# Weight halves, two written-out groups and another order of attention work in a fused attention and two-stage feed-forward kernel

## The chip, the cores and the metric

The kernel runs on one core of one Trainium2 chip. The metric is device time in microseconds (us) of one execution, as the median of several. Engines: TensorE (PE, its weight loads are PEld), VectorE (DVE), ScalarE (ACT), GpSimd (POOL) and the queue engine SyncE (SP), which starts transfers.

## The reference

Three computations follow each other, all in 32-bit floats, with the second kind of weights given as 64-bit words that the kernel turns into floats itself.

```python
# attention: batch 2, 8 heads, 768 positions, head size 64
scores = q @ k.T / sqrt(64) - slope[head] * distance
scores = where(key < n_global or 0 <= query - key < n_local, scores, -1e9)
a = softmax(scores); x = a @ v              # x: 1536 tokens x 512
# first feed-forward: 512 -> 2048 -> 512
h = x @ w_in; g = where(h > 0, h, exp(min(h, 0)) - 1); x = g @ w_out
# second feed-forward: 512 -> 768 -> 512
out = max(x @ w1, x @ w2, x @ w3) @ w_out2
```

## The kernel before, in words

**Precision.** Each large matrix product is done as three products of rounded operands: high by high, high by low and low by high part. So every operand is split into a high part (a cast, on ScalarE) and a low part (a subtraction, mostly on VectorE).

**Attention steps.** The attention is cut into 48 steps (k = 0 to 47): two heads, 128 queries, a window of at most 232 keys. `Windowed` (L117) holds their pieces: `scores_pe` (L214, products on TensorE into banks S0 and S1), `scores_dve` (L239, bias and minimum on VectorE), `scores_act` (L268, exponentials and sums on ScalarE), `sums` (L234), `recip` and `norm` (L263, L280, VectorE), `turn_pe` (L290, four transposes on TensorE into a bank), `turn_act` (L307, copy of the transposes to SBUF), `values_pe` (L318, products with the values). The finished values leave the bank by `values_high` and `values_low` (steps 0 to 15), by `pair_pe` and `pair_out` (two steps at once), or by `due_pe` and `due_out` (the steps that `due` names; for an even k these are k-3 and k-2).

**Weights.** The hidden layer of 2048 is cut into 16 groups of 128 (fc). The 64-bit words of a group (its columns of w_in and its rows of w_out, 2 x 512 words per partition) are turned into floats by six instructions: `c_rebase` (ScalarE), `c_low` (VectorE), `c_word` twice (VectorE), then the high part by `c_high` (ScalarE) and the low part by `c_rest` (VectorE). Here they are called rebase, low, word, word, high and rest. Half 0 is the w_in part and feeds the first product, half 1 the w_out part and feeds the output products. The last two groups arrive as separate halves.

**First stage.** `windowed` (L1182) runs steps 0 to 15 in a loop (L1221), which makes the first block of 512 tokens. From step 8 on each step also advances `convert`, a hand-written list of weight instructions for groups 0 and 1. In the steps named in `FILL` (L43) TensorE does that many identity products (`fill`, L759) whose result nobody reads. Behind the loop an epilogue written out by hand finishes steps 14 and 15, starts steps 16 and 17, and does the first product of group 0 in pieces.

**Main loop.** `run` (L765) then goes over three blocks of 512 tokens and in each over the 16 groups. In group fc TensorE does the product into bank h (`product`, 12 matmuls), some attention work of step k, and the output products of the group before (`out_high` 8 matmuls, `out_low` 4 matmuls, into banks y0 to y3). ScalarE and VectorE make e from h (`elu_exp`, `elu_max`) and split it into gh and gl (`high`, `low`). There is one bank h in blocks 0 and 1: the next product may start only when `elu_max` has read the last one. Step k goes with group k - 18: steps 18 to 33 with block 0, 34 to 47 with block 1, and block 2 has none. In block 0 the weights of group fc + 1 and fc + 2 are unpacked between the other instructions.

**What sets the order.** Nothing reorders the work: each engine takes its instructions in the order in which the program calls the methods above (a manual schedule), and waits where a tile isn't ready or a buffer not yet free. The eight PSUM banks are single tiles under the names h, S0, S1, TX and y0 to y3; a new tile in a bank waits for the last reader of the one before. Two tiles gl and gh, one tile e. In `run`, `joint` (L787) decides which of two orders a group uses for the attention step: if not joint, transposes of step k-1 directly behind the product, and values as pairs; if joint, `due_pe` directly behind the product, and the transposes later.

Of the kernel before, what the change touches and what calls it, by code (L numbers as in the profile page):

```python
# [12 lines left out]
F32 = mybir.dt.float32  # L13
# [5 lines left out]
ALU = mybir.AluOpType  # L19
# [5 lines left out]
P = 128  # L25
NB = S // P
NCC = DM // P
NFC = FF // P
# [370 lines left out]
class Feed:  # L399
# [54 lines left out]
    def c_rebase(self, c):  # L454
        for r, _ in self.parts(c):
            a = r[..., 1].bitcast(F32)
            self.nc.scalar.activation(a, a, AF.Copy, scale=2.0 ** -112)

    def c_low(self, c):
        for r, _ in self.parts(c):  # L460
# [4 lines left out]
    def c_word(self, c, n):  # L465
        v, op = ((3, ALU.logical_shift_left), (0x80000000, ALU.bitwise_and))[n]
        for r, _ in self.parts(c):
# [4 lines left out]
    def c_high(self, c):  # L472
        for r, h in self.parts(c):
            if c not in self.w:
                self.w[c] = self.wt.tile([P, 2, 2, 512], F32R, tag="w", name="w")
            self.nc.scalar.copy(self.w[c][:, h, 0], r[..., 0].bitcast(F32))  # L476

    def c_rest(self, c):
        for r, h in self.parts(c):
            w = self.w[c]  # L480
            self.nc.vector.tensor_tensor(
                w[:, h, 1], r[..., 0].bitcast(F32), w[:, h, 0].bitcast(F32), op=ALU.subtract
            )
        for d, k in ((self.whole, c), (self.wraw, 2 * c), (self.wraw, 2 * c + 1)):
            if c < NFC:
                d.pop(k, None)
# [277 lines left out]

    def run(self, at, k, x=None, h0=None, aside=None):  # L765

        nc, ps = self.nc, self.ps
# [7 lines left out]
        for bi, n in enumerate(BLOCKS):  # L777
            prev = y = None
            for fc in range(NFC):
                tag = ("h", "S0")[fc % 2] if k >= len(at.steps) + 2 else "h"  # L780
                if h0 is None:
                    h = ps.tile([P, 512], F32, tag=tag, name="h")[:, 0:n]
                    self.product(h, self.w[fc][:, 0], x, n, order=BEHIND if bi == 0 else None)
                else:
                    h, h0 = h0[:, 0:n], None
# [10 lines left out]
                if bi == 0:  # L796
                    self.c_word(fc + 1, 1)
                if left:
                    self.out_low(*left)
                late = bi == 0 or fc > 0  # L800
                if not late:
                    at.turn_act(k - 1, nc.vector.tensor_copy)
                    if k % 2 == 0:
                        at.pair_pe(k - 2)
                    at.scores_dve(k)
                    e = self.elu_exp(h, n)
                    at.scores_act(k)
                    if k % 2 == 0:
                        at.pair_out(k - 2, nc.scalar.copy)
                else:  # L810
                    ahead = bi == 0 and fc == NFC - 1
                    behind = joint and due and (ahead or k == len(at.steps))
                    if ahead:
                        at.scores_dve(k)
                        at.scores_act(k)
                        at.sums(k)
                        at.recip(k)
                        at.norm(k)
                    e = self.elu_exp(h, n)
# [4 lines left out]
                    if bi == fc == 0:  # L824
                        at.turn_act(k - 2, nc.scalar.copy)
# [4 lines left out]
                sooner = bi == 0 and (fc == 0 or k % 2)  # L830
                if sooner:
# [30 lines left out]
                if bi == nblk - 1 and fc == 7:  # L862
                    next(sums, None)
                if due and not behind:
                    at.turn_act(k - 1, nc.scalar.copy)
                if late and bi:
# [3 lines left out]
                    at.norm(k)  # L870
                if k % 2 == 0 and bi == fc == 0:
                    at.pair_pe(k - 2)
                    at.pair_out(k - 2, nc.scalar.copy)
                left = None
# [10 lines left out]
                if k % 2 == 0 and not joint and bi + fc:  # L885
                    at.pair_pe(k - 2)
                    at.pair_out(k - 2, nc.scalar.copy)
# [12 lines left out]
                k += 1  # L900
                prev = gh, gl
            if bi + 1 < nblk:
                t = [t] + [at.take(g0 + i) for i in range(1, BLOCKS[bi + 1] // GRP)]
# [278 lines left out]
def windowed(tc, ctx, io, flag):  # L1182
# [5 lines left out]
    with tc.manual_schedule():  # L1188
# [12 lines left out]
        def convert():  # L1201
            f.c_rebase(0)
            f.c_low(0)
            yield
            f.c_word(0, 0)
            f.c_rebase(1)
            yield
            f.c_word(0, 1)
            yield
            f.c_high(0)  # L1210
            f.c_low(1)
            yield
            f.c_rest(0)
            yield
            f.c_word(1, 0)
            yield
# [171 lines left out]
```

## Time and profile before

| | |
|---|---|
| Runs | 542.35, 542.89 and 542.96 us; median 542.89 |
| The profiled execution's own time | 542.19 us |
| Its span, first to last instruction | 540.4 us |
| Busy: TensorE, weight loads, VectorE, ScalarE, GpSimd | 530.7, 426.8, 393.7, 288.0, 82.9 us |
| Granted TensorE clock, mean over the span | 0.998 |
| First stage (steps 0 to 15 and epilogue) | about 0 to 44 us |
| Block 0, block 1, block 2 of the main loop | about 44 to 152, to 262, to 348 us |
| Second feed-forward | to 535 us |

In the lists of the profile a row gives a start, a duration, engine, line of the kernel, operation, written and read tiles, shapes and a count; a bracket at its end is the time that the engine sat idle before and who released it. Times are us from the span's start. A row's duration contains the start and the end of its instruction and overlaps with the next row of the same engine by some 0.08 to 0.1 us, so what an instruction costs its queue is read from one start to the next. The ends of matmuls are modelled. A fp32 product counts as two records.

### The profile page before, as it was taken

The numbers are of one execution on the slowest core, as the hardware profiler recorded it, in microseconds if no ns is written. First come the engines' busy times: TensorE is split into PE (matmuls) and PEld (weight loads), VectorE is DVE, ScalarE is ACT, GpSimd is POOL, SyncE is SP. The second block draws the span as 40 slices with busy tenths as digits, with TensorE's granted clock in tenths as the row PEclk, the third lists the DMA queues.
The fourth block names the chain that finished last, engine by engine and source line by source line (L and its number), as shares of the span: only waits on it lengthen the run. The fifth ranks groups of instructions, "written<-read, shape, count | busy, mean of one in ns | idle before, by whom it ended". The sixth has DMA issues, their size and how long they took to land.

```text
span 540.4 us, 7751 instructions
## 1 busy us (share of the span) xinstructions
PE 530.7 (98%) x2746; PEld 426.8 (79%) x2746; DVE 393.7 (73%) x828; ACT 288.0 (53%) x649; POOL 82.9 (15%) x89
## 2 busy tenths in 40 slices
PE   8999999999999999999999999999999999999995
PEld 6667787777777888888888888888888888888884
DVE  6889999999854444443567656787886989779883
ACT  5979877888845555554545655552157321224020
POOL 4220000000000000000000044321034410335000
PEclk9999999999999999999999999999999999999999
DMA  8929055442310111000000031331029301876014
GB/s 284 397 95 409 21 196 196 156 161 83 101 46 24 45 44 44 21 19 1 0 2 0 1 117 40 116 115 42 1 71 308 146 1 40 270 293 234 1 73 168
DMA packets 23455, 59.21 MB, mean 110 GB/s; under 512 B 2416, under 2 KB 2416, under 8 KB 23408
## 3 DMA queue, kind: packets, MB, share of 16 engines
q1 hardware_dynamic: 18368, 49.46, 26.5%
q10 hardware_dynamic: 5040, 9.18, 4.5%
q8 instruction: 24, 0.39, 0.3%
q14 instruction: 23, 0.19, 0.1%
HBM read 49.19 MB, written 9.44 MB: 108 GB/s over the span
## 4 chain that ended last, share of the span: by engine, by line
PE 91%; DVE 5%; ACT 3%; issue 0%; POOL 0%; ACTq 0%; POOLq 0%
PE h L674 26%; PE y L705 16%; PE y L713 8%; PE y L975 8%; PE y L1069 5%; PE y L674 5%; PE S L975 4%; PE TX L327 3%; PE TX L304 3%; PE S L228 3%; PE S L1069 2%; PE TX L975 2%; PE S L674 2%; PE h L975 2%; PE TX L1069 2%; ACT p L275 1%
## 5 line engine op out<-in xcount | busy, mean ns | idle before, releaser
L674 PE MATMUL h<-xh,w 128*128 128x512 f32 (+1 forms) x432 | 122.2, 387 | 0.2 <-ACT w L476 0.2
L705 PE MATMUL y<-gh,w 128*128 128x512 f32 x384 | 98.7, 399 | 0.1
L510 POOL TENSOR_TENSOR w<-wr,w 128x512 fp32r<-128x512 f32 x42 | 62.9, 1507 | 231.8 <-ACT w L509 220.5
L674 PEld LDWEIGHTS h<-xh,w 128*128 128x128 f32 x432 | 80.2, 188 | 17.9 <-ACT w L476 0.8
L705 PEld LDWEIGHTS y<-gh,w 128*128 128x128 f32 x384 | 69.7, 188 | 14.3 <-issue 0.5
L674 PE MATMUL h<-xl,w 128*128 128x512 f32 (+1 forms) x216 | 71.0, 386 | 0.0
L699 DVE SCALAR_TENSOR_TENSOR e<-e,h 128x512 f32<-128x512 f32 x48 | 32.9, 685 | 49.5 <-ACT e L695 49.4
L509 ACT CAST w<-wr 128x512 fp32r<-128x512 f32 x42 | 27.6, 663 | 63.4 <-DVE wr L500 51.1
L694 ACT ACTIVATE e<-h 128x512 f32<-128x512 f32 x48 | 28.7, 599 | 55.3 <-PE h L674 51.2
L275 ACT ACTIVATE p<-p,m 128x232 f32<-128x232 f32 (+1 forms) x96 | 44.9, 471 | 17.1 <-DVE m L254 16.9
L713 PE MATMUL y<-gl,w 128*128 128x512 f32 x192 | 51.6, 390 | 0.0
L500 DVE SCALAR_TENSOR_TENSOR wr<-wr 128x512 uint32<-128x512 uint32 x48 | 44.2, 921 | 7.5 <-ACT wr L492 6.0
L686 DVE TENSOR_TENSOR gl<-e,gh 128x512 fp32r<-128x512 f32 x48 | 33.1, 689 | 19.9 <-ACT gh L681 19.9
L674 PEld LDWEIGHTS h<-xl,w 128*128 128x128 f32 x216 | 40.4, 188 | 8.1 <-issue 0.2
L198 POOL TENSOR_SCALAR raw<-raw,qsc 128x256 f32<-128x256 f32 x24 | 16.8, 699 | 193.4 <-DMA raw<-qk 193.4
L975 PE MATMUL y<-t,w 128*128 128x512 f32 x180 | 42.7, 389 | 0.0
L713 PEld LDWEIGHTS y<-gl,w 128*128 128x128 f32 x192 | 36.0, 188 | 8.0 <-issue 0.3
L681 ACT CAST gh<-e 128x512 fp32r<-128x512 f32 x48 | 29.6, 616 | 23.5 <-DVE e L699 23.3
L468 DVE SCALAR_TENSOR_TENSOR wr<-wr 128x1024 uint32<-128x1024 uint32 (+1 forms) x36 | 39.8, 1120 | 0.4
L975 PEld LDWEIGHTS y<-t,w 128*128 128x128 f32 x180 | 33.8, 188 | 7.0
L695 ACT ACTIVATE e<-e 128x512 f32<-128x512 f32 x48 | 30.3, 632 | 1.5
L985 ACT CAST g<-m 128x512 fp32r<-128x512 f32 x18 | 10.9, 621 | 35.2 <-DVE m L1004 27.0
(155 smaller groups left out, 837.5 us busy)
## 6 DMA issues: line engine op xcount, KB each, us to landing
wr<-wa SPq DMA_DIRECT2D x14, 1024.0 KB, 6.9
wr<-wb SPq DMA_DIRECT2D x24, 512.0 KB, 4.6
v<-v SPq DMA_DIRECT2D x24, 256.0 KB, 2.8
part<-row ACTq DMA_DIRECT2D x24, 256.0 KB, 4.6
raw<-qk SPq DMA_DIRECT2D x16, 312.0 KB, 4.6
row<-part SPq DMA_DIRECT2D x12, 256.0 KB, 3.1
out<-rows ACTq DMA_DIRECT2D x11, 256.0 KB, 2.3
raw<-qk SPq DMA_DIRECT2D x8, 260.0 KB, 4.7
```

The lines of the kernel that those rows point to most:

```text
L275: self.nc.scalar.activation(p[:, o], p[:, o], AF.Exp, bias=m[:, u:u + 1], scale=-1.0, accum_out=m[:, 2 + u:3 + u],)
L468: self.nc.vector.scalar_tensor_tensor(r[..., 0], r[..., 1], v, r[..., 0], op0=op, op1=ALU.bitwise_or)
L500: self.nc.vector.scalar_tensor_tensor(t, a, c, t, op0=op, op1=ALU.bitwise_or)
L510: nc.gpsimd.tensor_tensor(w[:, u, 1], v, w[:, u, 0].bitcast(F32), op=ALU.subtract)
L674: nc.tensor.matmul(out[:, o:n], w[:, part % 2, c * P:c * P + P], (xl if part == 2 else xh)[:, c, o:n], start=(c, part) == order[0], stop=( ...
L686: (engine or self.nc.vector).tensor_tensor(gl[:, 0:n], e[:, 0:n], gh[:, 0:n].bitcast(F32), op=ALU.subtract)
L695: self.nc.scalar.activation(e, e, AF.Exp, scale=-1.0)
L699: self.nc.vector.scalar_tensor_tensor(e, e, -1.0, h, op0=ALU.add, op1=ALU.max)
L705: self.nc.tensor.matmul(y[e][:, 0:n], w[:, a, e * P:e * P + P], g[0][:, 0:n], start=fc == 0 and a == 0, stop=False,)
L713: self.nc.tensor.matmul(y[e][:, 0:n], w[:, 0, e * P:e * P + P], g[1][:, 0:n], start=False, stop=fc == NFC - 1,)
L975: self.nc.tensor.matmul(out, w[:, u, i % 2, b + c * P:b + c * P + P], o[:, i // 2, c], start=c == i == 0, stop=c == 1 and i == 2,)
L1069: nc.tensor.matmul(o, t[:, a, r], w[:, u, b], start=u == k == 0, stop=u == 1 and k == 2,)
```

## The change

It has four parts.

1. `FILL`: one identity product in place of two in each of steps 8 to 13.
2. The methods `c_...` take a half h. `convert` now unpacks half 0 of groups 0 and 1 first and of half 1 of group 0 only the first instructions; it has eight pieces, one for each of steps 8 to 15. The other pieces of half 1 stand in the epilogue and in `begin`.
3. `begin` is new: groups 0 and 1 of the first block written out by hand in place of the first two turns of the loop in `run`. The product of group 1 goes to bank y3; its first four matmuls stand before the transposes of step 17, the other eight behind them. `run` begins at group 2 with step 20.
4. `joint` is now true for every group of blocks 0 and 1 (before: for groups 2 to 15 of each block). What changes by it are groups 0 and 1 of block 1: the values of step 32 alone directly behind the product, scores, and then the transposes of step 33.

```diff
-FILL = {1: 2, 2: 2, 8: 2, 9: 2, 10: 2, 11: 2, 12: 2, 13: 2}
+FILL = {1: 2, 2: 2, 8: 1, 9: 1, 10: 1, 11: 1, 12: 1, 13: 1}
...
-    def parts(self, c):
-
+    def parts(self, c, h=None):
+
+        hs = slice(0, 2) if h is None else slice(h, h + 1)
         if c in self.whole:
-            return [(self.whole[c], slice(0, 2))]
+            return [(self.whole[c][:, hs], hs)]
         return [(self.wraw[j], j % 2) for j in (2 * c, 2 * c + 1) if j in self.wraw and c < NFC]
...
-    def c_low(self, c):
-        for r, _ in self.parts(c):
+    def c_low(self, c, h=None):
+        for r, _ in self.parts(c, h):
             self.nc.vector.tensor_scalar(
...
+    def begin(self, at, k, x, h):
+
+
+        copy, n = self.nc.scalar.copy, BLOCKS[0]
+        w = self.w[1][:, 0]
+        at.load_values(k)
+        self.w_ahead(4)
+        at.scores_pe(k, m=2)
+        at.turn_pe(k - 2, "y2")
+        h1 = self.ps.tile([P, 512], F32, tag="y3", name="h1")
+        self.product(h1, w, x, n, 0, 0, 4, BEHIND)
+        at.recip(k - 1)
+        at.norm(k - 1)
+        self.c_low(1, 1)
+        at.turn_pe(k - 1)
+        self.product(h1, w, x, n, 0, 4, 8, BEHIND)
+        e = self.elu_exp(h, n)
+        at.turn_act(k - 2, copy)
+        at.turn_act(k - 1, copy)
+        self.elu_max(e, h)
+        at.scores_dve(k)
+        gh = self.high(e, n)
+        gl = self.low(e, gh, n)
+        prev = gh, gl
+        self.c_high(0, 1)
+        self.c_rebase(2)
+        self.c_low(2)
+        self.c_rest(0, 1)
+        self.c_word(2, 0)
+        at.pair_pe(k - 2)
+        e = self.elu_exp(h1, n)
+        self.elu_max(e, h1)
+        at.scores_act(k)
+        at.sums(k)
+        at.pair_out(k - 2, copy)
+        y = self.out_tiles()
+        self.out_high(y, 0, prev, n)
+        self.out_low(y, 0, prev, n)
+        self.c_word(2, 1)
+        at.recip(k)
+        at.norm(k)
+        self.c_high(2)
+        k += 1
+        at.turn_pe(k - 1)
+        at.turn_act(k - 1, copy)
+        at.scale_queries(k // 2 + 1)
+        at.load_pair(k // 2 + 2)
+        self.w_ahead(6)
+        self.c_rest(2)
+        at.scores_dve(k)
+        at.scores_act(k)
+        at.sums(k)
+        gh = self.high(e, n)
+        self.c_word(1, 0, 1)
+        self.c_word(1, 1, 1)
+        self.c_high(1, 1)
+        self.c_rebase(3)
+        at.recip(k)
+        at.norm(k)
+        gl = self.low(e, gh, n)
+        self.c_rest(1, 1)
+        self.c_low(3)
+        self.c_word(3, 0)
+        return y, (gh, gl)
...
-            prev = y = None
-            for fc in range(NFC):
+            y, prev = begun or (None, None)
+            for fc in range(2 if begun else 0, NFC):
...
-                joint = fc > 1
+                joint = bi < 2
...
+                late = bi == 0 or fc > 0
+                if not late:
+                    at.due_out(due, nc.vector.tensor_copy)
+                    if joint:
+                        at.turn_pe(k - 1)
                 if left:
                     self.out_low(*left)
-                late = bi == 0 or fc > 0
                 if not late:
                     at.turn_act(k - 1, nc.vector.tensor_copy)
-                    if k % 2 == 0:
-                        at.pair_pe(k - 2)
                     at.scores_dve(k)
                     e = self.elu_exp(h, n)
                     at.scores_act(k)
-                    if k % 2 == 0:
-                        at.pair_out(k - 2, nc.scalar.copy)
...
         def convert():
-            f.c_rebase(0)
-            f.c_low(0)
+            f.c_rebase(0, 0)
+            f.c_low(0, 0)
             yield
-            f.c_word(0, 0)
-            f.c_rebase(1)
+            f.c_word(0, 0, 0)
+            f.c_rebase(1, 0)
             yield
-            f.c_word(0, 1)
+            f.c_word(0, 1, 0)
+            f.c_low(1, 0)
             yield
-            f.c_high(0)
-            f.c_low(1)
+            f.c_high(0, 0)
+            f.c_word(1, 0, 0)
             yield
-            f.c_rest(0)
+            f.c_rest(0, 0)
+            f.c_rebase(0, 1)
             yield
-            f.c_word(1, 0)
+            f.c_word(1, 1, 0)
+            yield
+            f.c_high(1, 0)
+            f.c_low(0, 1)
+            yield
+            f.c_rest(1, 0)
             yield
...
+        f.c_word(0, 0, 1)
         at.scores_pe(k, m=2)
...
+        f.c_rebase(1, 1)
         at.scores_act(k)
         at.scores_dve(k + 1, True)
         at.values_low(k - 2, x)
+        f.c_word(0, 1, 1)
...
-        at.turn_pe(k, tags[k % 3])
-        at.recip(k + 1)
-        at.norm(k + 1)
         for _ in words:
             pass
-        f.run(at, first + 2, x, h, lambda: covered(nc, at.const, ni, flag))
+        begun = f.begin(at, k + 2, x, h)
+        f.run(at, first + 4, x, begun, lambda: covered(nc, at.const, ni, flag))
```

## Rows read from the trace of the kernel before


**Rows 1.** Chain that ended last, first stage and first block: start, us, what.

```profile
29.74 1.13 DVE w L481
...
32.55 0.62 PE y L304 x4
...
53.10 3.05 PE h L674 x12
56.16 0.59 PE TX L327 x8
56.74 0.98 PE S L228 x8
...
61.10 2.73 PE h L674 x12
63.83 0.44 PE TX L304 x4
...
67.04 2.77 PE h L674 x12
```

**Rows 2.** Windows of 5 us: busy us of each engine (instructions), clock, DMA.

```profile
35.00:40.00 5.00, 5.00 (x48) 3.65 (x46) 3.24 (x16) 2.87 (x12) 0.00 (x0) 1.00 0.04 11
40.00:45.00 5.00, 4.54 (x42) 3.52 (x43) 3.83 (x16) 4.92 (x17) 0.00 (x0) 1.00 1.02 409
```

**Rows 3.** Timeline of VectorE, then ScalarE, one step each: start, us, instruction.

```profile
25.98 0.39 DVE L254 CUSTOM_DVE_ANT_0 p<-y,rel 128x232 f32<-128x232 f32 x1
...
27.52 0.69 DVE L461 TENSOR_SCALAR wr<-wr 128x1024 uint32<-128x1024 uint32 x1
...
24.27 0.59 ACT L315 COPY p<-y 116x512 f32<-116x512 f32 x1
...
25.95 0.58 ACT L315 COPY p<-y 116x512 f32<-116x512 f32 x1
```

**Rows 4.** Timeline of VectorE, late weight groups, whose halves are unpacked apart.

```profile
135.49 1.29 DVE L481 TENSOR_TENSOR w<-wr,w 128x512 fp32r<-128x512 f32 x2
...
138.00 2.49 DVE L468 SCALAR_TENSOR_TENSOR wr<-wr 128x512 uint32<-128x512 uint32 x4
```

**Rows 5.** Timeline of VectorE: scores of step 8 and of step 14.

```profile
18.18 0.40 DVE L254 CUSTOM_DVE_ANT_0 p<-S,rel 128x232 f32<-128x232 f32 x1 [0.34 <-PE S L228]
...
33.46 0.39 DVE L254 CUSTOM_DVE_ANT_0 p<-S,rel 128x232 f32<-128x232 f32 x1
```

**Rows 6.** Timeline of TensorE: first transposes after group 0's product.

```profile
42.85 0.62 PE L304 MATMUL y<-ident,p 128*116 128x128 f32 x4
```

**Rows 7.** Timeline of TensorE: identity products of a step, transposes of a later one.

```profile
24.42 0.71 PE L762 MATMUL z<-ident 128*128 128x128 f32 x4
...
27.66 0.65 PE L304 MATMUL TX<-ident,p 128*116 128x128 f32 x4 [0.27 <-DVE xl L343]
```

**Rows 8.** Windows of 2 us over 18 to 34: the least busy of eight.

```profile
32.00:34.00 2.00, 1.45 (x14) 1.13 (x15) 2.00 (x6) 1.22 (x6) 1.57 (x1) 1.00 0.00 0
```

**Rows 9.** Timeline of VectorE, then ScalarE; the wait before stands in brackets.

```profile
43.25 0.17 DVE L266 RECIPROCAL m<-m 128x2 f32<-128x2 f32 x1 [0.29 <-ACT m L237]
...
58.46 0.39 DVE L254 CUSTOM_DVE_ANT_0 p<-S,rel 128x232 f32<-128x232 f32 x1
...
62.73 2.48 DVE L468 SCALAR_TENSOR_TENSOR wr<-wr 128x1024 uint32<-128x1024 uint32 x2
...
79.21 0.69 DVE L699 SCALAR_TENSOR_TENSOR e<-e,h 128x512 f32<-128x512 f32 x1 [0.44 <-ACT e L695]
...
65.50 1.13 ACT L476 CAST w<-wr 128x1024 fp32r<-128x1024 f32 x1
```

**Rows 10.** Timeline of VectorE and TensorE at the second block's start.

```profile
154.91 0.69 DVE L315 COPY p<-TX 116x512 f32<-116x512 f32 x1 [1.96 <-PE TX L304]
...
156.53 0.68 DVE L699 SCALAR_TENSOR_TENSOR e<-e,h 128x512 f32<-128x512 f32 x1
...
157.93 1.66 PE L674 MATMUL h<-xh,w 128*128 128x512 f32 x6
```

More of the change, by code (lines that the diff above doesn't have):

```diff
@@ L446, in w_ahead, with c_rebase @@
             self.w_load()
-    def parts(self, c):
+    def parts(self, c, h=None):
+        hs = slice(0, 2) if h is None else slice(h, h + 1)
         if c in self.whole:
-            return [(self.whole[c], slice(0, 2))]
+            return [(self.whole[c][:, hs], hs)]
         return [(self.wraw[j], j % 2) for j in (2 * c, 2 * c + 1) if j in self.wraw and c < NFC]
-    def c_rebase(self, c):
-        for r, _ in self.parts(c):
+    def c_rebase(self, c, h=None):
+        for r, _ in self.parts(c, h):
             a = r[..., 1].bitcast(F32)
             self.nc.scalar.activation(a, a, AF.Copy, scale=2.0 ** -112)
-    def c_low(self, c):
-        for r, _ in self.parts(c):
+    def c_low(self, c, h=None):
+        for r, _ in self.parts(c, h):
             self.nc.vector.tensor_scalar(
@@ L463, in c_low, with c_word @@
             )
-    def c_word(self, c, n):
+    def c_word(self, c, n, h=None):
         v, op = ((3, ALU.logical_shift_left), (0x80000000, ALU.bitwise_and))[n]
-        for r, _ in self.parts(c):
+        for r, _ in self.parts(c, h):
             self.nc.vector.scalar_tensor_tensor(
@@ L470, in c_word, with c_high, c_rest @@
             )
-    def c_high(self, c):
-        for r, h in self.parts(c):
+    def c_high(self, c, h=None):
+        for r, hs in self.parts(c, h):
             if c not in self.w:
                 self.w[c] = self.wt.tile([P, 2, 2, 512], F32R, tag="w", name="w")
-            self.nc.scalar.copy(self.w[c][:, h, 0], r[..., 0].bitcast(F32))
-    def c_rest(self, c):
-        for r, h in self.parts(c):
+            self.nc.scalar.copy(self.w[c][:, hs, 0], r[..., 0].bitcast(F32))
+    def c_rest(self, c, h=None):
+        for r, hs in self.parts(c, h):
             w = self.w[c]
             self.nc.vector.tensor_tensor(
-                w[:, h, 1], r[..., 0].bitcast(F32), w[:, h, 0].bitcast(F32), op=ALU.subtract
+                w[:, hs, 1], r[..., 0].bitcast(F32), w[:, hs, 0].bitcast(F32), op=ALU.subtract
             )
+        if h == 0:
+            return
         for d, k in ((self.whole, c), (self.wraw, 2 * c), (self.wraw, 2 * c + 1)):
@@ L762, in fill, with run @@
             self.nc.tensor.matmul(t[:, 0:P], z, z, start=True, stop=True)
-    def run(self, at, k, x=None, h0=None, aside=None):
+    def begin(self, at, k, x, h):
[60 more added lines that the diff above has]
+        return y, (gh, gl)
+    def run(self, at, k, x=None, begun=None, aside=None):
         nc, ps = self.nc, self.ps
@@ L777, in run @@
         for bi, n in enumerate(BLOCKS):
-            prev = y = None
-            for fc in range(NFC):
+            y, prev = begun or (None, None)
+            for fc in range(2 if begun else 0, NFC):
                 tag = ("h", "S0")[fc % 2] if k >= len(at.steps) + 2 else "h"
[L781 to L785, printed above, removed]
+                h = ps.tile([P, 512], F32, tag=tag, name="h")[:, 0:n]
+                self.product(h, self.w[fc][:, 0], x, n, order=BEHIND if bi == 0 else None)
                 at.load_values(k)
-                joint = fc > 1
+                joint = bi < 2
                 due = at.due(k) if joint else []
@@ L823, in run @@
                             at.turn_pe(k - 1)
-                    if bi == fc == 0:
-                        at.turn_act(k - 2, nc.scalar.copy)
                     if not due:
@@ L829, in run @@
                     next(sums, None)
-                sooner = bi == 0 and (fc == 0 or k % 2)
+                sooner = bi == 0 and k % 2
                 if sooner:
@@ L863, in run @@
                     next(sums, None)
-                if due and not behind:
+                if due and late and not behind:
                     at.turn_act(k - 1, nc.scalar.copy)
@@ L870, in run @@
                     at.norm(k)
-                if k % 2 == 0 and bi == fc == 0:
-                    at.pair_pe(k - 2)
-                    at.pair_out(k - 2, nc.scalar.copy)
                 left = None
@@ L884, in run @@
                     at.turn_act(k - 1, nc.scalar.copy)
-                if k % 2 == 0 and not joint and bi + fc:
+                if k % 2 == 0 and not joint:
                     at.pair_pe(k - 2)
@@ L901, in run @@
                 prev = gh, gl
+            begun = None
             if bi + 1 < nblk:
```

## The prediction, made before the changed kernel was run

> **What bounds the kernel now.** I read the page first: it marks TensorE busy nearly throughout, and a busy TensorE can hide short waits. So I turn to the chain that ended last. Up to 32.4 us it runs on VectorE (unpacked weights, as L481), changes to TensorE at 32.55, goes back to ScalarE and VectorE between 40 and 53, and from 53.10 on names TensorE alone: product, values, scores, transposes, output products, next product [rows 1]. What TensorE has lost by 53.10 is lost for good, and from there the time is its work, unless another engine begins to hold it up. The windows of 5 us name the candidate: VectorE is busy 3.24 and 3.83 of 5 between 35 and 45 [rows 2], and after that it does not stop: from the reciprocal of step 17 at 43.25 to the scores of step 20 at 58.46 its queue never waits [rows 9]. The first block is bound twice, by TensorE and, a hair behind, by VectorE. The reader should watch VectorE's place in its queue rather than TensorE's busy share.
>
> **Steps 8 to 13: shorter.** Without weights a step takes VectorE 1.54 us (25.98 to 27.52) and ScalarE 1.68 (24.27 to 25.95) [rows 3]. The weights come on top. Whole pieces hold VectorE 0.60 (low, a row of 0.69 that overlaps the next one [rows 3]), 1.14 to 1.20 (word, two in 2.48 [rows 9]) and 1.13 (rest [rows 1]). Half pieces I take from the last groups, which come as halves: four words in 2.49, so 0.60 each, two rests in 1.29, also 0.60 [rows 4]; for a half low 0.34. Two halves cost 0.0 to 0.1 us more than a whole; I add 0.06 for each pair.
> [...]
> Before, the weights on VectorE in steps 8 to 13 are low, word, word, low, rest, word: 6 x 1.54 + 5.84 = 15.1, and the scores of step 14 start 15.28 after those of step 8 [rows 5], so the queue explains it all. After, they are 0.34, 0.60, 0.94, 0.60, 0.60, 0.60, and VectorE needs 12.9. ScalarE gets half a rebase or high (0.55, half of L476's 1.13 [rows 9]) in four of the six, 2.23 there. The longer queue of each step gives 13.5, VectorE alone 12.9; I take 13.3. **Step 14 comes 2.0 us sooner.** TensorE's chain then runs through its own transposes, values and products as before, from 32.55 to the end of group 0's product at 42.85 [rows 1, 6]. Of the 2.0, 0.4 goes at once, because the chain starts from VectorE's step 13, and 0.2 where half a rebase now stands on ScalarE ahead of the product's last operand: 41.4 in place of 42.85, **1.4 sooner**.
>
> **The identity products.** Two hold TensorE at most 0.71 us, so the six that go are worth at most 6 x 0.35 = 2.1. I cost them at nothing: the transposes behind them wait for VectorE anyway (27.66, released by xl) [rows 7]. If that cover is gone, as the steps are now shorter, they give up to 0.3 in each of two steps. [...]
>
> **The two written-out groups.** Their worth is where VectorE stands when the run goes back into the loop. Before, the stretch from 43.25 to 58.46 is 15.2 us of unbroken work [rows 9]. After: (a) that reciprocal comes 1.15 sooner, at 42.1. (b) Work moved behind this point: low 0.34, two words 1.20 and two rests 1.20, all halves, in place of a word and a rest of 2.28, so +0.46. The other halves fall into the 2.93 us that VectorE is idle between 35 and 45 [rows 2] and cost nothing. (c) A new wait. ScalarE copies the transposes of step 17 before it makes gh of group 0, and those transposes stand on TensorE behind scores (0.98), the transposes of step 16 (0.44) and the first four of group 1's twelve products (4 x 2.73/12 = 0.91) [rows 1]: 41.4 + 2.33 + 0.44 = 44.2. The copy (0.58 [rows 3]) ends near 44.8, gh near 45.4. VectorE has done the scores of step 18 by 44.5, and its next instruction is gl, which needs gh: **0.9 us idle**. Behind gl wait low and word of group 2, the last rest of group 0, and the max that frees the bank of group 1. (d) After step 18's norm it waits again, 0.45, for group 2's high on ScalarE. Sum: -1.15 + 0.46 + 0.9 + 0.45 = +0.65. VectorE reaches the scores of step 20 at 59.1, **0.65 us late**, though TensorE comes to group 2's product at 51.3, 1.8 sooner than 53.10.
> TensorE can't keep the 1.8. Group 3 starts when group 2's max has freed its bank, about 60.4 against 61.10. Group 4 needs its high part, which ScalarE makes from 65.50 to 66.63, behind the second word (65.13) [rows 9]; 0.65 later the words end at 65.8 and the part at 66.9, and the product starts there in place of 67.04 [rows 1]. **Of the 1.8 TensorE has 0.1 left.** Its chain has no gap afterwards, so that stays; VectorE catches up unseen (at 79.21 it waits 0.44 for e [rows 9]). Bounds: without (c) the part ends at 66.0 and 1.0 is gained; with (c) twice as long it ends at 67.8 and 0.75 is lost. Loads and the scaling of queries keep their order on SP and POOL; no load is issued later than before.
>
> **The second block's joint order.** Before, its group 0 runs product, transposes of step 33, scores, the first block's low products, values of 32 and 33. VectorE copies the transposes from 154.91, the max that frees the product's only bank ends at 157.21, and TensorE comes for that bank at 157.93, 0.7 later [rows 10]. After, the values of step 32 (0.59) and the scores (0.98) stand ahead of the transposes (0.44) [rows 1]: from the product's end (154.91 less the 0.44 of the transposes, 154.4) these are done at 156.45, the copy at 157.1, the two score instructions at 157.8, the max at 158.4. TensorE is there at 157.4 and **waits 1.0 us**, and the values of step 33 are still to come, some 0.4 beside those of step 34. That is 158.45 against 157.93, plus 0.4: 0.9 late. Bounds 0 (if the bank is not what decides) and 0.9; nearest is the copy that waits for its transposes, so I take **+0.6**. ScalarE is spared one copy that nothing waits for.
>
> **Sum.** -0.1 + 0.6 = +0.5 on the profiled execution, whose span is 540.4 and whose own time was 542.19, 0.7 under the median of 542.89. Against the median that is **543.4 us**, +0.1%. A measurement of this kernel can tell about 0.2%, 1.1 us, from no change, so the forecast is no difference that can be measured.
>
> **The rivals.**
> *The shorter steps carry whole (faster).* The place is steps 8 to 13, the price their 2.0 us. It decides if VectorE comes to the scores of step 20 before 58.0, since TensorE then starts group 4 a microsecond and more before 67.04. For it: TensorE is 1.8 ahead at group 2, and VectorE had 2.9 us to fill [rows 2]. Against: VectorE is the second bound of the block, and the halves add to its work. It gains 2.0 and pays 0.6: 541.5. Chance 0.28.
> *gh comes late (slower, the other side).* The place is the copy of step 17's transposes, which stands on ScalarE ahead of gh, while VectorE stands at gl with six instructions behind it. Each microsecond more that these transposes wait for TensorE is paid once, since the first block has no room on VectorE; it decides from scores of step 20 at 59.6 on. With an idle of 1.8 in place of 0.9: +0.75 + 0.6, 544.2. For it: from 43.25 to 58.46 VectorE had no gap [rows 9]. Against: only four products stand ahead. Chance 0.20.
> *The bank is free in time (same).* The second block's order costs nothing; -0.1: 542.8. Chance 0.12.
> *The clock falls (slower).* [...] Against it stands 1.00 at 1.45 of 2.00 [rows 8]. Chance 0.03. [...]
> The forecast keeps 0.37.
>
> **The numbers.** Faster is the first rival, 0.28; same the forecast and the free bank, 0.49; slower the late gh and the clock, 0.23. The forecast's own range, from its bounds, is 542.2 to 544.2. Cases of both signs hold about half, so the range is 541.5 to 544.5: it reaches to the middle of the fast case and past that of the slow one, and leaves out the clock and the outer halves, under 0.2.
>
> **What would show it.** Right: the scores of step 14 near 31.5; about 1 us of idle on VectorE ahead of a gl near 45, released by gh; the scores of step 20 near 59; group 4's product within 0.5 of 67.0, released by L476; near 155 to 158 a wait of TensorE for L699. Wrong: scores of step 20 before 58 (then (c) or (d) failed, and the kernel is faster) or after 59.6; group 4's product more than a microsecond from 67.0. A granted clock under 1.00 before 50 us would point to the identity products.

## The result: slower by half a per cent, and the profile after

The changed kernel takes 545.99 us (median of 6 runs, 545.48 to 546.57) against 542.91 for the kernel before in the same series (542.35 to 544.01): a ratio of 1.0057 [1.0044, 1.0069], 3.1 us more, outside the predicted range. The profiled execution took 546.12 us, with a span of 544.2. Lines of the code have moved a little: the product is now L677 (L674), the output products L708 and L716, the elu's max L702 (L699), gl L689, gh L684, the second word L469, rest L482, high L477, rebase L458, low L462.

The page hardly tells the two kernels apart. Its busy times of the engines and its row of the clock:

```profile
PE 531.7 (98%) x2734; PEld 426.3 (78%) x2734; DVE 395.8 (73%) x837; ACT 288.3 (53%) x652; POOL 81.0 (15%) x89
...
PEclk9999899999999999999999999999999999999999
```

A single 8 in the clock, in the fifth slice (54 to 68 us), is all that it shows. So I laid the chains that ended last side by side. That of the changed kernel, first stage and first block (start, us, what):

```profile
31.34 0.62 PE y L304 x4
...
41.35 0.71 PE h L677 x3
...
44.55 0.45 PE TX L304 x4
45.03 0.59 ACT p L315
45.61 0.53 ACT gh L684
46.16 0.69 DVE gl L689
...
54.67 0.87 DVE wr L469
...
58.65 0.84 PE TX L304 x4
59.49 3.23 PE y L708 x8
...
63.65 2.74 PE h L677 x12
...
69.61 2.50 PE h L677 x11
```

Before, TensorE is alone on the chain from 53.10 on [rows 1]. Now VectorE stays on it up to 58 us, and group 3's product starts at 63.65 in place of 61.10, group 4's at 69.61 in place of 67.04, 2.57 late. That lag is still 2.63 at the block's last product (145.78 against 143.15) and 2.64 at group 0 of the second block (154.35 against 151.71). The second loss comes there. The chain of the changed kernel at that place:

```profile
154.35 2.72 PE h L677 x12
...
158.64 0.59 PE TX L304 x4
...
159.25 0.04 DVE p L315
...
160.58 0.61 DVE e L702
...
161.24 3.04 PE h L677 x12
...
175.55 2.72 PE h L677 x12
```

From the start of group 0's product to that of group 3 it takes 175.55 - 154.35 = 21.20 us, before 171.85 - 151.71 = 20.14: 1.06 more. 2.64 and 1.06 make the 3.7 us that remain (a late product on the chain starts at 367.23 against 363.51). The times of the two profiled executions differ by 3.93 (546.12 and 542.19) and the medians by 3.1, because the profiled execution of the kernel before was 0.7 under its median.

VectorE's timeline shows each step that was forecast:

```profile
18.25 0.40 DVE L254 CUSTOM_DVE_ANT_0 p<-S,rel 128x232 f32<-128x232 f32 x1
...
31.70 0.40 DVE L254 CUSTOM_DVE_ANT_0 p<-S,rel 128x232 f32<-128x232 f32 x1
...
42.61 0.17 DVE L266 RECIPROCAL m<-m 128x2 f32<-128x2 f32 x1 [0.29 <-ACT m L237]
...
46.16 0.69 DVE L689 TENSOR_TENSOR gl<-e,gh 128x512 fp32r<-128x512 f32 x1 [1.08 <-ACT gh L684]
...
52.17 1.23 DVE L482 TENSOR_TENSOR w<-wr,w 128x1024 fp32r<-128x1024 f32 x1 [0.54 <-ACT w L477]
...
53.95 1.59 DVE L469 SCALAR_TENSOR_TENSOR wr<-wr 128x512 uint32<-128x512 uint32 x2
...
60.55 0.39 DVE L254 CUSTOM_DVE_ANT_0 p<-S,rel 128x232 f32<-128x232 f32 x1
```

Steps 8 to 14 take 13.45 us in place of 15.28 [rows 5], as forecast. The wait for gh (1.08) and the wait for group 2's high (0.54) are both there. But from the reciprocal of step 17 to the scores of step 20, the stretch that I will use to compare all runs, VectorE takes 60.55 - 42.61 = 17.94 us in place of 15.21 [rows 9].

Something was not forecast at all: TensorE waited 1.83 us for a bank. Its timeline, and windows of 1 us around it:

```profile
58.65 0.84 PE L304 MATMUL TX<-ident,p 128*116 128x128 f32 x4 [1.83 <-ACT xraw L390]
```

```profile
57.00:58.00 1.00, 0.00 (x0) 0.00 (x0) 1.00 (x2) 0.97 (x3) 0.00 (x0) 1.00 0.00 0
58.00:59.00 1.00, 0.35 (x3) 0.35 (x4) 0.90 (x2) 0.60 (x2) 0.00 (x0) 0.99 0.00 0
59.00:60.00 1.00, 1.00 (x5) 0.90 (x4) 0.97 (x2) 0.00 (x0) 0.00 (x0) 0.50 0.00 0
...
62.00:63.00 1.00, 1.00 (x5) 0.80 (x4) 1.00 (x2) 0.97 (x6) 0.00 (x0) 0.81 0.00 0
```

The transposes of step 19 go into bank TX, which still holds the values of steps 16 and 17 until ScalarE copies them out (`due_out`, L390). That copy stands on ScalarE behind the rebase of group 3 and the two exponentials of group 2's e, and starts at 58.35. Behind the wait the clock, the third number from the right, falls from 1.00 to 0.50 for three windows, and the eight matmuls of `out_high` take 3.23 us where they take 1.85 elsewhere on the same chain. So there were three suspects: VectorE's lateness, the bank with the fall of the clock behind it, and the second block's order.

### The profile page after: what moved, and what is told of

Read it like the earlier page. It is cut to its first block, busy times and chain, and to the rows that moved or that the text cites. A ratio compares the mean times of both kernels' runs of the same rounds, so it can differ in the third digit from the quotient of the medians.

```text
span 544.2 us, 7742 instructions
## 1 busy us (share of the span) xinstructions
PE 531.7 (98%) x2734; PEld 426.3 (78%) x2734; DVE 395.8 (73%) x837; ACT 288.3 (53%) x652; POOL 81.0 (15%) x89
## 4 chain that ended last, share of the span: by engine, by line
PE 91%; DVE 5%; ACT 3%; issue 1%; POOL 0%; DVEq 0%; ACTq 0%; POOLq 0%
PE h L677 26%; PE y L708 16%; PE y L716 8%; PE y L1036 7%; PE y L1130 5%; PE y L677 4%; PE S L1036 4%; PE TX L304 3%; PE TX L327 3%; PE S L228 3%; PE S L1130 2%; PE TX L1036 2%; PE S L677 2%; PE h L1036 2%; PE TX L1130 1%; DVE p L288 1%
## 5 line engine op out<-in xcount | busy, mean ns | idle before, releaser
L677 PE MATMUL h<-xh,w 128*128 128x512 f32 (+1 forms) x432 | 122.3, 387 | 1.2 <-DVE e L702 1.1
L708 PE MATMUL y<-gh,w 128*128 128x512 f32 x384 | 100.7, 404 | 0.4 <-DVE e L702 0.3
L677 PEld LDWEIGHTS h<-xh,w 128*128 128x128 f32 x432 | 80.2, 188 | 18.7 <-DVE e L702 1.5
L708 PEld LDWEIGHTS y<-gh,w 128*128 128x128 f32 x384 | 70.7, 191 | 15.7 <-DVE e L702 0.7
L677 PE MATMUL h<-xl,w 128*128 128x512 f32 (+1 forms) x216 | 71.1, 386 | 0.0
L702 DVE SCALAR_TENSOR_TENSOR e<-e,h 128x512 f32<-128x512 f32 x48 | 32.9, 686 | 50.2 <-ACT e L698 50.0
L716 PE MATMUL y<-gl,w 128*128 128x512 f32 x192 | 51.6, 390 | 0.0
L689 DVE TENSOR_TENSOR gl<-e,gh 128x512 fp32r<-128x512 f32 x48 | 33.1, 690 | 21.0 <-ACT gh L684 20.3
L677 PEld LDWEIGHTS h<-xl,w 128*128 128x128 f32 x216 | 40.4, 188 | 8.2 <-issue 0.2
L198 POOL TENSOR_SCALAR raw<-raw,qsc 128x256 f32<-128x256 f32 x24 | 14.8, 618 | 199.0 <-DMA raw<-qk 171.2
L716 PEld LDWEIGHTS y<-gl,w 128*128 128x128 f32 x192 | 36.0, 188 | 7.8
L684 ACT CAST gh<-e 128x512 fp32r<-128x512 f32 x48 | 29.6, 616 | 23.4 <-DVE e L702 23.2
L469 DVE SCALAR_TENSOR_TENSOR wr<-wr 128x1024 uint32<-128x1024 uint32 (+1 forms) x40 | 40.8, 1033 | 0.5
L288 DVE TENSOR_SCALAR p<-p,m 128x232 f32<-128x232 f32 (+1 forms) x96 | 28.8, 342 | 1.7
```

Source lines behind the costliest of these rows:

```text
L288: nc.vector.tensor_scalar(p[:, o], p[:, o], m[:, 6 + u:7 + u], None, op0=ALU.mult)
L469: self.nc.vector.scalar_tensor_tensor(r[..., 0], r[..., 1], v, r[..., 0], op0=op, op1=ALU.bitwise_or)
L677: nc.tensor.matmul(out[:, o:n], w[:, part % 2, c * P:c * P + P], (xl if part == 2 else xh)[:, c, o:n], start=(c, part) == order[0], stop=( ...
L689: (engine or self.nc.vector).tensor_tensor(gl[:, 0:n], e[:, 0:n], gh[:, 0:n].bitcast(F32), op=ALU.subtract)
L702: self.nc.vector.scalar_tensor_tensor(e, e, -1.0, h, op0=ALU.add, op1=ALU.max)
L708: self.nc.tensor.matmul(y[e][:, 0:n], w[:, a, e * P:e * P + P], g[0][:, 0:n], start=fc == 0 and a == 0, stop=False,)
```

## The experiments

The ratios are to runs of the kernel before on the same chip in the same series, whose medians lie between 542.83 and 543.19. The stretch is step 17's reciprocal to step 20's scores on VectorE; group 4 is the start of its product; b1 is groups 0 to 3 of the second block. The profiled executions start the first transposes of L304 at 9.2 to 9.8 us, so where starts of two runs are compared below, that start is subtracted or its difference is named.

| Run | Median us | Ratio | Stretch | Group 4 | b1 |
|---|---|---|---|---|---|
| the kernel before | 542.9 | | 15.21 | 67.04 | 20.14 |
| the changed kernel | 545.99 | 1.0057 [1.0044, 1.0069] | 17.94 | 69.61 | 21.20 |
| old joint order | 545.41 | 1.0041 [1.0027, 1.0055] | 17.94 | 70.21 | 20.25 |
| copy first | 545.86 | 1.0050 [1.0036, 1.0063] | 17.87 | 68.63 | 21.21 |
| gh first | 544.83 | 1.0031 [1.0019, 1.0042] | 17.14 | 68.02 | 21.19 |
| all three | 543.50 | 1.0006 [0.9997, 1.0015] | 17.07 | 67.96 | 20.14 |
| early rebase | 545.68 | 1.0052 [1.0040, 1.0064] | 18.15 | 69.28 | 21.19 |
| before + one identity product | 543.17 | 1.0001 [0.9992, 1.0010] | 15.39 | 67.79 | 20.16 |
| before + new joint order | 543.84 | 1.0016 [1.0007, 1.0025] | 15.20 | 67.26 | 21.23 |
| halves, old loop | 542.34 | 0.9986 [0.9977, 0.9995] | 15.48 | 66.89 | 20.21 |
| the same, two identity products | 542.70 | 0.9992 [0.9983, 1.0001] | 15.45 | 67.02 | 20.14 |
| halves, old loop, early rebase | 541.71 | 0.9978 [0.9970, 0.9987] | 15.49 | 65.90 | 20.14 |
| the same, early word | 541.93 | 0.9981 [0.9972, 0.9989] | 15.12 | 66.04 | 20.17 |

**Old joint order in the changed kernel.**

```diff
-                joint = bi < 2
+                joint = fc > 1 or bi == 0
...
+                    if k % 2 == 0:
+                        at.pair_pe(k - 2)
...
```

> The changed kernel with the second block's old order for its groups 0 and 1 (transposes of step 33 directly behind the product, values of 32 and 33 as a pair). Theory: the new order makes TensorE wait for the bank of the product, and between group 15 of block 0 and group 3 of block 1 the changed kernel loses 1.06 us more than the kernel before (2.63 late to 3.70 late). Then this kernel is 1.0 to 1.1 us faster than the changed one, near 544.9 us, and its product of group 1 in block 1 starts 2.6 after the one of before in place of 3.24. Rival: the second block only shows a wait that would come anyway, and the time stays at 546.0.

Measured 1.0041. The chain of this run at the second block:

```profile
154.98 2.72 PE h L677 x12
...
175.23 2.72 PE h L677 x12
```

20.25 us in place of 21.20: the boundary's loss is gone in the trace, 0.95. In the time 0.16% (0.9 us) is gone, though the intervals of the two ratios overlap. **New joint order in the kernel before** tells it apart better:

```diff
-                joint = fc > 1
+                joint = fc > 1 or bi == 1
...
+                    at.due_out(due, nc.vector.tensor_copy)
+                    if joint:
+                        at.turn_pe(k - 1)
...
```

> The kernel before with the new joint order in groups 0 and 1 of the second block and nothing else. Theory (the joint order costs by itself what the boundary shows): from group 0 to group 3 of the second block 21.2 us in place of 20.14, and the time 543.9 (543.7 to 544.1). Rival (it costs only because the changed kernel comes to the boundary late): the same time as before, 542.9.

The ratio is 1.0016 [1.0007, 1.0025], 0.9 us, and TensorE's timeline shows the same wait as in the changed kernel, where the row reads [1.10 <-DVE e L702]:

```profile
158.80 1.67 PE L674 MATMUL h<-xh,w 128*128 128x512 f32 x6 [1.10 <-DVE e L699]
```

So the order of the second block costs 0.9 to 1.1 by itself, however early the kernel comes there.

**The copy that frees bank TX first**, ahead of group 2's exponentials, with the rebase of group 3 moved up so that ScalarE is free for it:

```diff
         at.turn_act(k - 1, copy)
+        self.c_rebase(3)
...
-        self.c_rebase(3)
...
+                    first = bi == 0 and fc == 2
+                    if first:
+                        at.due_out(due, nc.scalar.copy)
                     e = self.elu_exp(h, n)
...
```

> The changed kernel, in which ScalarE does two things sooner: the rebase of group 3 stands ahead of the scores of step 19, where ScalarE had 0.97 us of idle, and in group 2 the copy that frees bank TX stands ahead of the exponentials. Theory: TensorE's wait of 1.83 us ahead of the transposes of step 19 and the half clock behind it are the first loss; without them group 3's product moves from 63.65 to 61.9, where VectorE's max frees its bank, and group 4's from 69.61 to 68.5, where VectorE and ScalarE have its high part ready. So 1.1 us faster than the changed kernel, near 544.9. Rival one: VectorE's lateness alone sets group 4, and the time stays at 546.0. Rival two: TensorE's wait and the clock are the whole loss of the first block, and 2.5 us come back, 543.5.

In time the first rival was right, 545.86 and a ratio of 1.0050. In the trace the theory was: group 4 at 68.63, where 68.5 was forecast. TensorE's timeline:

```profile
56.89 0.65 PE L304 MATMUL TX<-ident,p 128*116 128x128 f32 x4
...
62.08 0.47 PE L677 MATMUL h<-xh,w 128*128 128x512 f32 x1 [1.69 <-DVE e L702]
```

The wait for the bank is gone and the granted clock reads 1.00 in every window from 54 to 65 us. TensorE runs ahead, and then waits 1.69 for the max of group 2's e, which stands on VectorE behind the scores of step 20. Group 4 starts at 68.63, with the start of the first stage subtracted 1.36 later than before. So in this profile VectorE alone costs 1.4, and the bank and the clock add 1.2 in the trace of the changed kernel. Of these, 0.94 are left at the end: from the first transposes to the last instruction on VectorE the changed kernel takes 530.03 us and this run 529.09. But what follows that instruction lasts 4.8 to 5.4 us in six profiles of this case, and over the runs the two kernels differ by 0.07% (0.4 us), with intervals that allow anything from nothing to more than 1 us.

The mean clocks of the runs say a little more. A stretch like the one at 59 us takes an estimated 0.003 off the mean (three windows at 0.50 and one at 0.81, in a span of 544.2 us), so four of the six runs of the changed kernel, with a mean of 0.999, had none like it; their median is 545.85, no longer than with the copy first. So the wait for the bank costs nothing that can be seen where the clock stays. The other two runs (546.12, the profiled one, and 546.57) have a mean of 0.996. Only the first is known to have had the stretch: the clock also falls behind the last product, where no product is left to slow: in the profile of the kernel before it reads 0.93 from 537 us and 0.50 from 538 to the end at 540.4, and TensorE has no instruction from 535 on. The profiled run of gh first below has a mean of 0.996 with 1.00 in every window from 54 to 65 us.

**gh of group 0 ahead of the copy of step 17's transposes** on ScalarE:

```diff
         at.turn_act(k - 2, copy)
-        at.turn_act(k - 1, copy)
         self.elu_max(e, h)
         at.scores_dve(k)
         gh = self.high(e, n)
+        at.turn_act(k - 1, copy)
         gl = self.low(e, gh, n)
```

> The changed kernel with gh of group 0 made on ScalarE ahead of the copy of step 17's transposes. VectorE's idle ahead of the first gl should fall from 1.08 us to under 0.2, and the scores of step 20 come a microsecond sooner, near 59.6 in place of 60.55. Theory: TensorE's wait for bank TX goes over ScalarE and stays, group 3's product stays near 63.6 and the time within 0.4 of 546.0. Rival (VectorE's place alone decides, as the prediction had it): 1.0 us faster, 545.0.

The rival was right: 544.83, a ratio of 1.0031, 1.4 us less by the ratios. VectorE's timeline:

```profile
42.86 0.17 DVE L266 RECIPROCAL m<-m 128x2 f32<-128x2 f32 x1 [0.30 <-ACT m L237]
...
45.39 0.69 DVE L689 TENSOR_TENSOR gl<-e,gh 128x512 fp32r<-128x512 f32 x1
...
60.00 0.39 DVE L254 CUSTOM_DVE_ANT_0 p<-S,rel 128x232 f32<-128x232 f32 x1
```

The idle time before gl is gone, the stretch takes 0.80 less, and group 4 comes 0.75 sooner than with the copy first (the first stage's start subtracted in both); the 1.4 us are more than that, but no more than the intervals of the two ratios allow. TensorE still waits 1.74 for bank TX here, and this time the clock stays at 1.00.

**All three at once.** The edits are the three above.

> The changed kernel with all three edits at once: the second block's old joint order, the copy that frees bank TX issued first, and gh ahead of the copy of step 17's transposes. Theory (three separate causes that add): the joint order gives back 0.95 (by the boundary in the trace of the old-joint run), gh first gives back about 1.0 (the scores of step 20 some 0.9 sooner in its trace), and with the copy first no TensorE wait in front of the transposes of step 19 and no stretch at half clock, which is worth up to 0.5 in the median: 543.5 to 544.1, still 0.6 to 1.1 over the kernel before, because VectorE stays some 1.2 us late at step 20. Rival (the causes overlap, and VectorE's place alone decides in the first block): the copy first gives nothing beside gh first, 543.9 to 544.2. Rival (the half convert is what costs): no better than 544.8.

543.50, a ratio of 1.0006 [0.9997, 1.0015]. By the ratios the three give 0.16 + 0.07 + 0.26 = 0.49% one by one and 0.51% together, so the theory that they add holds, within intervals of 0.1% each. TensorE's wait for bank TX is gone here, and yet group 4 comes only 0.06 sooner than with gh first alone (67.96 against 68.02, the first stages start alike). The stretch is still 17.07, 1.9 longer than before: the two written-out groups are left, with half pieces of groups 0 and 1 behind step 17, 0.54 us of idle time before the rest of group 2 and 0.27 before its first word.

**The half rebase of group 1 one copy earlier** in the changed kernel, in ScalarE's idle time ahead of that copy:

```diff
+        f.c_rebase(1, 1)
         at.turn_act(k - 1, nc.scalar.copy)
         at.values_high(k - 2, x)
-        f.c_rebase(1, 1)
```

> The changed kernel with the half rebase of group 1 issued one copy earlier on ScalarE, in its 1.29 us of idle time near 37.5 us, and nothing else. Theory (this half rebase is why group 0's product came 0.86 and not 1.4 us sooner, and the reciprocal of step 17 0.64 and not 1.15; VectorE's place passes on to group 3): group 0's product ends 0.5 sooner, the scores of step 20 come 0.5 sooner, and the time is 545.5. Rival (gh still waits behind ScalarE's copies, whatever comes before): the scores of step 20 where they were, and 546.0.

1.0052, between theory (545.5) and rival (546.0). The first half of the theory holds: the last matmuls of group 0's product follow without a gap, and the reciprocal of step 17 starts at 42.07, 0.54 sooner. But the scores of step 20 come only 0.33 sooner (60.22; the first stage starts 0.08 later here, which goes on top of both): the idle time before gl grows from 1.08 to 1.25 us. What is gained ahead of a fixed wait is partly lost in it.

**One identity product in the kernel before.**

```diff
-FILL = {1: 2, 2: 2, 8: 2, 9: 2, 10: 2, 11: 2, 12: 2, 13: 2}
+FILL = {1: 2, 2: 2, 8: 1, 9: 1, 10: 1, 11: 1, 12: 1, 13: 1}
```

> The kernel before with one identity product in place of two in steps 8 to 13 and nothing else. Theory (the identity products lie in TensorE's waits, and in those steps VectorE and ScalarE set the pace): the same time, 542.7 to 543.1, and steps 8 to 14 still take 15.3 us. Rival (they delay the product's matmuls): steps 8 to 14 shorter by 0.14 each, 0.8 in all, and the time 542.3 or less. Rival (they hold TensorE's clock): a stretch under full clock before 35 us, and the time 543.5 or more.

1.0001 [0.9992, 1.0010]: no difference that these runs can show. Steps 8 to 14 did not get shorter, the scores go from 18.59 to 34.23, 15.64 us; why that is 0.36 more than before I did not test.

**The halves alone**: the convert in halves with one identity product, no `begin`, the old loop from group 0 and the old joint order. The half pieces that are left follow in group 0's turn of the loop.

```diff
...
-                    self.c_rest(fc + 1)
+                    if half:
+                        self.c_rest(0, 1)
+                    self.c_rest(fc + 1, half)
...
-            f.c_rebase(0)
-            f.c_low(0)
+            f.c_rebase(0, 0)
+            f.c_low(0, 0)
...
+        f.c_word(1, 0, 1)
+        f.split = True
...
```

> The kernel before with two parts of the change alone: the halves in the first stage and one identity product in place of two. Groups 0 and 1 run in the old loop, the second halves of both are unpacked in the epilogue and beside group 0, the second block keeps its order. Theory: steps 8 to 13 take 13.4 us in place of 15.28, of which 0.8 is left at the end of group 0's product; VectorE then has the same work as before and no new wait, so all of the first block starts 0.6 to 0.9 sooner: 542.1 us. Rival: the eight additional instructions on VectorE and the half pieces on ScalarE eat it up, 542.9 or later.

It is a little faster than the kernel before, 0.9986 [0.9977, 0.9995]. **With two identity products** in steps 8 to 13:

> The kernel with the convert in halves, the old loop from group 0 and the old joint order, with two identity products in steps 8 to 13 in place of one. Theory (identity products lie in waits, halves alone shorten the steps): 542.3 to 542.5, and steps 8 to 14 take 13.5 us as with one. Rival (the shorter steps leave no room for the second product): steps 8 to 14 longer by 0.14 a step, 14.2 us, and 542.9.

0.9992 [0.9983, 1.0001], within the other's interval. VectorE's scores of steps 8 and 14, first with one product, then with two:

```profile
18.60 0.40 DVE L254 CUSTOM_DVE_ANT_0 p<-S,rel 128x232 f32<-128x232 f32 x1 [0.34 <-PE S L228]
...
31.96 0.39 DVE L254 CUSTOM_DVE_ANT_0 p<-S,rel 128x232 f32<-128x232 f32 x1
```

```profile
18.69 0.40 DVE L254 CUSTOM_DVE_ANT_0 p<-S,rel 128x232 f32<-128x232 f32 x1 [0.21 <-PE S L228]
...
32.10 0.39 DVE L254 CUSTOM_DVE_ANT_0 p<-S,rel 128x232 f32<-128x232 f32 x1
```

13.36 and 13.41 us: the halves shorten the steps, the identity products do nothing to them.

**The halves with the early rebase.** The edit is that of the early rebase above, in this kernel.

> The kernel with halves, the old loop from group 0 and the old joint order, with the half rebase of group 1 issued one copy earlier on ScalarE, in its 1.29 us of idle time. Theory (this half rebase holds up the last xh tile and with it the end of the first stage): group 0's product ends 0.5 sooner and the time is 0.5 less than that kernel's, a ratio to the kernel before of 0.9977. Rival (VectorE's words in front of the first elu set the pace): no change, 0.9986.

0.9978 [0.9970, 0.9987], 541.71 us: the fastest of all, 1.1 us under the kernel before. In the chain of the kernel with halves alone the rebase stands between the cast of an xh tile and the exponentials:

```profile
39.60 0.27 ACT xh L337
39.86 0.60 ACT wr L459
40.47 0.92 ACT p L275 x4
...
66.89 2.77 PE h L678 x12
```

With the early rebase it is off the chain:

```profile
39.16 0.27 ACT xh L337
39.43 0.95 ACT p L275 x4
...
65.90 2.77 PE h L678 x12
```

Here no wait follows that could eat the gain: group 4 starts 0.99 sooner, of which 0.29 is an earlier start of the first stage. **And a half word of group 1 moved forward** into VectorE's idle time near 41 us:

```diff
         f.c_low(1, 1)
+        f.c_word(1, 0, 1)
...
-        f.c_word(1, 0, 1)
```

> The same with the half word of group 1 moved from behind the last steps into VectorE's 0.44 us of idle time near 41 us as well. Theory (VectorE's chain from step 17 on passes on to every group of the first block): its half word of 0.68 us leaves the chain, the scores of step 20 come 0.6 sooner than with the early rebase alone, and the time is 0.5 less again, a ratio of 0.9968. Rival (what VectorE gains there TensorE or ScalarE take up before group 3): a ratio of 0.9975 or more.

0.9981 [0.9972, 0.9989], no better: the rival was right. The word stands ahead of the last xl tile, TensorE waits 0.30 us for that tile, and the reciprocal of step 17 comes 0.49 later. The stretch is 0.37 shorter, and that only makes up for it.

## Why the prediction was wrong

**"Steps 8 to 13: shorter"** was right: 13.3 was forecast, 13.45 came, and 13.36 with the halves alone.

**"1.4 sooner"** for the end of group 0's product was too much: the last three matmuls start at 41.35 and end near 42.0 against 42.85 [rows 6], 0.86 sooner. The half rebase on ScalarE, which I priced at 0.2, stands ahead of the exponentials of steps 16 and 17 as well as of the last operand, and cost VectorE's reciprocal of step 17 some 0.54 (early rebase). So VectorE started the stretch 0.64 sooner and not 1.15.

**"The identity products"** at nothing: right, by two pairs of runs.

**"The two written-out groups"** had the right steps and too small a sum. Each term, forecast against measured: (a) -1.15 against -0.64; (b) moved work +0.46 against +0.77, because the two half words of group 1 take 1.50 us from start to start and not the 1.20 that I took from the last groups [rows 4], where neighbouring words belong to different halves (0.60 each), while here the second reads what the first has just written (0.72 for the first) and GpSimd works at the same time (0.78 for the second; what the rows say of that stands in the last section); (c) the wait for gh 0.9 against 1.08; (d) the wait for the high part 0.45 against 0.54, and some 0.2 more before the words of group 3, which read what the low right ahead of them writes (0.79 from the start of that low to theirs, 0.60 from the start of group 2's to the rest behind it), with 0.15 in small gaps. The sum was to be +0.65 and is 2.09 (60.55 against 58.46), past the 59.6 that the prediction named as its refutation. The step that failed is this sum, and through it "of the 1.8 TensorE has 0.1 left". The 1.8 themselves were not there either: the product of group 2 starts at 52.19 on TensorE and not at 51.3, 0.9 sooner than before. The slack that this sentence grants was about right: with the scores of step 20 1.93 late, group 4 comes 1.36 late (copy first, where the clock stays), with 1.17 it comes 0.61 late (gh first; the first stage's start subtracted in both), so some 0.6 is hidden, and +0.65 would have cost next to nothing. The rival "gh comes late" had the right sign, its condition came true (scores of step 20 past 59.6), and its time was 544.2; but its mechanism, an idle of 1.8 in place of 0.9, is only part of it: the four terms grew together. Since they are all on VectorE's queue, they had one direction; bounds from one of them alone (c) were too narrow.

**"TensorE waits 1.0 us ... 0.9 late"**: the wait is 1.10, and the loss 1.06 in the trace, where I took 0.6 as the nearer of bounds 0 and 0.9. The working gave 0.9, and the copy for whose sake I discounted it [rows 10] says nothing of the size. The rival "the bank is free in time" fell.

**Missed**: bank TX. I followed the new order through VectorE and did not ask which copy on ScalarE frees the bank that the transposes of step 19 write. "The clock falls" was placed in steps 8 to 13, where the traces do not show it: with one identity product a step the granted clock reads 1.00 in every window of 2 us from 18 to 34, in the changed kernel and in the kernel before with that edit alone. It fell elsewhere, behind this wait: this trace shows 0.50 once, at 59 us, behind a gap of 1.83 us. Yet copy first, which takes both away, changes the time by no more than its interval can tell.

By the ratios, each with an interval of about 0.1 to either side, the change is made up of: the halves in the old loop -0.14%, what is left of the written-out groups +0.20 (all three against halves with the old loop), gh behind the copy +0.26, bank TX +0.07, the second block's order +0.16: +0.55% of the +0.57 measured.

## What to carry to other kernels

Time gained in a stage ahead of a shared queue is worth only what the place behind it can pass on, so follow the engine that is second in line, instruction by instruction, to the point where the old order is resumed, and add up every wait with its own error in the same direction. When work is written out by hand, list for each bank and tile which instruction frees it and what stands ahead of that on its engine, the copies too. A change of several parts is best tried part by part: here the part that saved time was hidden under two that together lost more.

## What the hardware showed that was not expected

Two half words cost more than one whole one, and not by one price: 1.20 us a pair in the last groups [rows 4], 1.33 from start to start with the halves alone, 1.50 at 53.95 in the changed kernel, against 1.13 to 1.15 for a whole word. Two half rests cost 1.20 against 1.13 (halves alone). No run was made to tell the words apart, but the rows do so in two steps. In the last groups neighbouring words work on different halves, and each takes 0.60. Where the second word follows the first on the same half and reads its result, the first takes 0.72 or 0.73; whole words show the same, 1.25 to 1.27 for the first of two. The second takes 0.61 (a row of 0.69) or about 0.8 (a row of 0.87), and that goes with GpSimd, which scales queries (L198) at that time. Changed kernel, then gh first:

```profile
54.11 0.88 POOL L198 TENSOR_SCALAR raw<-raw,qsc 128x256 f32<-128x256 f32 x1 [21.91 <-DMA raw<-qk]
54.67 0.87 DVE L469 SCALAR_TENSOR_TENSOR wr<-wr 128x512 uint32<-128x512 uint32 x1
```

```profile
54.27 0.69 DVE L469 SCALAR_TENSOR_TENSOR wr<-wr 128x512 uint32<-128x512 uint32 x1
54.30 1.01 POOL L198 TENSOR_SCALAR raw<-raw,qsc 128x256 f32<-128x256 f32 x1 [21.86 <-DMA raw<-qk]
```

In the changed kernel GpSimd's instruction starts while the first word runs and ends 0.34 behind it, and the second word, which starts in that time, ends 0.55 behind GpSimd's. With gh first GpSimd's starts while the second word runs, ends 0.35 behind it, and the word's row is 0.69 long. The row of both words is 1.59 to 1.61 long in four profiles (changed kernel, old joint order, copy first, early rebase) and 1.42 in two (gh first, all three). GpSimd's own rows are 0.88 and 1.01 long here, where the median of its 24 rows in the changed kernel is 0.51. Whether the one engine holds up the other no run tested, and GpSimd's times are rough. If it does, 0.17 (1.59 less 1.42) of the 0.80 that gh first took off the stretch is owed to GpSimd and not to gh.

And TensorE's clock did not answer alike to alike waits: behind bank TX it fell to 0.50 in the profiles of the changed kernel (wait 1.83 us), of the old joint order (1.84) and of the early rebase (1.90), and stayed at 1.00 with gh first (1.74). What decides between the two, these runs don't tell.
